# Hop of a transposed copy moved from its output to its input, with whole first loads on two queues and a new instruction order

## The chip, the cores and the metric

The kernel runs on one core of one Trainium2 chip. The metric is the device time of one execution in microseconds. The kernel before is known by three runs and by one profiled execution, from which all durations come.

## What is computed

The reference is a gated linear recurrence over 768 steps for 4 batches and 8 heads of 48 channels, followed by a two-layer network on the 3072 resulting rows of 384 channels.

```
f = 1.0 / (1.0 + np.exp(-f_logit))
state = np.zeros((B, H, D, D))
for t in range(S):                       # S = 768, D = 48
    state = f[:, :, t, :, None] * state + np.einsum('bhd,bhe->bhde', k[:, :, t], v[:, :, t])
    y[:, :, t] = np.einsum('bhd,bhde->bhe', q[:, :, t], state)
x = y.transpose(0, 2, 1, 3).reshape(B * S, H * D)
h = x @ w_in                             # 384 x 2048
out = np.maximum(0.01 * h, h) @ w_out    # 2048 x 384
```

All inputs and the output are float32; the kernel computes in bfloat16 with float32 sums.

## The kernel before

**Units.** The sequence is cut into 6 chunks of 128 steps; a chunk of one batch is a unit, so there are 24 units, numbered chunk by chunk (units 0 to 3 are the first chunks of the four batches). Within a unit the recurrence becomes matmuls: the log gates are summed by a triangular matrix (`gate_pe`), k and q are scaled by exponentials of these sums (`decay_em`, `decay_a`, `k_scale`, `q_scale`), both are transposed on TensorE (`turn_pe`) and copied out of PSUM (`turn_k`, `turn_q`), multiplied into scores (`score_pe`), masked (`mask_dve`), multiplied with v and with the state of the chunk before (`mix_pe`), and the state is carried on (`state_pe`, `state_dve`, `state_pool`). The result goes out of PSUM (`y_out`), is transposed (`x_pe`, `x_out`) into `xT`, and the network follows per pair of units: `up` (w_in, eight calls of 6 matmuls a pair, into PSUM), `up_act` (leaky ReLU on ACT into `gT`), `down` (w_out) and `put`, which copies the rows out of PSUM and stores them. For the first four units `down_cols` and `put_cols` do the second layer in two halves of the columns of w_out.

**The first chunks.** Units 0 to 3 are done together, in a layout of their own whose helpers begin with `q_`. Partition 32 groups of 4 steps by 4 batches: partition p holds batch p % 4, and four consecutive steps j lie in one row. `load_quad` (L67) loads f, k and q of one batch into every fourth partition. The heads are done in two halves hh of four. `q_turn_pe` (L211) transposes the scaled k or q into a PSUM bank; there the columns lie in the order pair of heads, j, group of steps t, batch b. `kTq` and `qTq` want them as pair of heads, batch, step (t, j). `q_turn_out` (L217) makes the two access patterns of the copy between them, and `q_k_out` and `q_q_out` run it through `move` on VectorE (L140) or ScalarE (L138), one copy of 128 x 512 for each half of heads and pair pp. `q_score_pe` (L228) reads the copies of both pairs of one half; `q_mask`, `q_wf_act` with `q_mask_pool`, `q_mix_pe`, `y_out`, `x_pe` and `x_out` follow. `q_back_pe` turns k back for the state.

**Order.** The order is written out by hand as one long list of calls; no scheduler moves anything. Each call puts its instructions at the end of the queue of its engine (V is VectorE or DVE, A is ScalarE or ACT, G is GpSimd or POOL), and each engine runs its queue in order. All loads (`load_part`, L155) and all outputs (`put`, `put_cols`) are issued by SyncE's queue (SP), in order as well, so a load that stands behind an output is issued only when that output's data are ready. The weights (`load_w_in` in four parts, `load_w_out` in two halves) are issued by POOL and converted to bfloat16 on the way. Raw loads have rings of six buffers. Each load or output by SP or ACT also waits for the one eight places earlier to have landed. `idle_pe(n, bank)` (L130) issues n matmuls on zeros whose result nobody reads. PSUM has eight banks; the last number of a call is its bank.

In the list before, the four calls of `load_part(4, ...)` are followed on SP by `put_cols(0, 0, 1)`, the load of f of unit 5, `put_cols(1, 0, 2)`, and the loads of k, q and v of unit 5. The first `up` calls are `up(0, 0, 7)`, `up(0, 1, 5)` and `up(0, 5, 4)`; eleven `up` stand ahead of the first `down_cols`.

Of the kernel before, what the change touches and what calls it, by code (L numbers as in the profile page):

```python
# [9 lines left out]
FP32 = mybir.dt.float32  # L10
# [6 lines left out]
def kernel(  # L17
# [45 lines left out]
    fq = [const.tile([128, 4, 4, D], FP32, name=f"fq{i}", tag=f"fq{i}") for i in range(2)]  # L63
    kq = const.tile([128, H, 4, D], FP32, tag="kq")
    qq = [const.tile([128, 4, 4, D], FP32, name=f"qq{i}", tag=f"qq{i}") for i in range(2)]

    def load_quad(eng, t, src, b, lo, n):  # L67
        eng.dma_start(out=t[b::4, :, :, :].rearrange("p h j d -> p h (j d)"),
                      in_=src[b, lo:lo + n, 0:C, :].rearrange("h (t j) d -> t h (j d)", j=4))
# [12 lines left out]

    nc.scalar.preload_act_table_set("natural_log_exp_and_others")
# [27 lines left out]
    qhs = [const.tile([128, H, 64], BF16, name=f"qh{i}", tag=f"qh{i}") for i in range(3)]  # L111
    khs = [const.tile([128, H, 64], BF16, name=f"kh{i}", tag=f"kh{i}") for i in range(4)]
# [12 lines left out]
    for t in lfs + khs + qhs:  # L125
        nc.vector.memset(t[:, :, D:64], 0.0)
    for t in state_b:
        nc.vector.memset(t, 0.0)
# [19 lines left out]
    turned = {name: ring(name, 3, [128, P2, 128], BF16) for name in ("kT", "qT")}  # L148
# [36 lines left out]
    def q_exp_act(hh):  # L185
        nc.scalar.activation(fq[hh], fq[hh], AF.Exp, scale=-1.0)

    def q_ln_act(hh):
        nc.scalar.activation(lfq[hh][:, :, :, 0:D], fq[hh].rearrange("p h j d -> p j h d"), AF.Ln, bias=1.0)
# [18 lines left out]
    def q_q_scale(eng, hh, a):  # L208
        q_scale_half(eng, qhq, qq[hh], aq, hh, a)
# [104 lines left out]
    def q_scale(u):  # L314
        r = raw[u]
        nc.gpsimd.tensor_mul(qhs[u % 3][:, :, 0:D], r["q"], a_ts[u % 3])  # L316
# [4 lines left out]
    def turn_pe(u, bk):  # L321
        tp = bank16(bk).rearrange("p (i a n) -> p i a n", i=2, a=P2)
        for i, src in enumerate((khs[u % 4], qhs[u % 3])):
            for p in range(P2):
                nc.tensor.transpose(tp[:, i, p, :], src[:, 2 * p:2 * p + 2, :], ident)  # L325

# [112 lines left out]
    idle_pe(31, 7)  # L439
# [3 lines left out]
    q_gate_pe(0, 0, 0)  # L443
    q_gate_pe(0, 1, 1)
    q_ln_act(1)
    idle_pe(3, 7)
    q_decay_act(0, 1, emq, 1.0, 1)
    q_end_pe(2)
    q_gate_pe(1, 0, 3)
    q_decay_act(0, 0, emq, 1.0, 0)  # L450
    q_k_scale(V, 0, 1)
    q_end_act(2)
    q_k_scale(V, 0, 0)
    q_gate_pe(1, 1, 4)
    q_decay_act(0, 0, aq, -1.0, 0)
    q_decay_act(0, 1, aq, -1.0, 1)
    q_q_scale(V, 0, 0)
    q_turn_pe(khq, 0, 0, 5)
    q_turn_pe(khq, 0, 1, 5)
    q_decay_act(1, 1, emq, 1.0, 4)  # L460
    q_q_scale(G, 0, 1)
    q_turn_pe(qhq, 0, 0, 6)
    q_k_out(V, 0, 0, 5)
    idle_pe(4, 7)
    q_decay_act(1, 1, aq, -1.0, 4)
    q_decay_act(1, 0, emq, 1.0, 3)
    q_k_scale(G, 1, 1)
    q_k_out(V, 0, 1, 5)
    q_turn_pe(qhq, 0, 1, 6)
    idle_pe(7, 7)  # L470
    q_decay_act(1, 0, aq, -1.0, 3)
    q_k_scale(V, 1, 0)
    q_q_out(A, 0, 0, 6)
    q_q_scale(G, 1, 0)
    cast_v(V, 0)
    q_turn_pe(khq, 1, 0, 7)
    q_q_out(A, 0, 1, 6)
    q_turn_pe(khq, 1, 1, 7)
    q_q_scale(V, 1, 1)
    load_w_in(0)  # L480
    q_turn_pe(qhq, 1, 0, 2)
    q_k_out(V, 1, 0, 7)
    q_score_pe(0, 1, 0, 1)
    load_w_in(1)
    q_turn_pe(qhq, 1, 1, 2)
    q_wf_act(0, 1, 0, 0)
    q_k_out(V, 1, 1, 7)
    q_score_pe(0, 0, 4, 5)
    cast_v(G, 1)
    idle_pe(2, 6)  # L490
    q_q_out(A, 1, 0, 2)
    cast_v(G, 2)
    q_mask(0, 1, 1, 1)
    q_back_pe(3, 3)
    idle_pe(6, 7)
    q_mask_pool(0, 1, 0)
    q_q_out(A, 1, 1, 2)
    q_mask(0, 0, 1, 5)
    q_score_pe(1, 0, 6, 0)
    q_mask(0, 0, 0, 4)  # L500
    idle_pe(3, 7)
    load_w_in(2)
    q_mask(1, 0, 0, 6)
    q_score_pe(1, 1, 7, 1)
    load_w_in(3)
    idle_pe(7, 5)
    q_wf_act(1, 1, 1, 1)
    load_w_out(0)
    q_mask(1, 0, 1, 0)
    q_wf_act(1, 1, 0, 7)  # L510
    q_back_out(V, 3, 3)
    q_mix_pe(0, 2)
    q_mask_pool(1, 1, 1)
    q_mix_pe(1, 5)
    q_back_pe(0, 4)
    y_out(A, 0, 2)
    y_out(V, 1, 5)
    idle_pe(2, 7)
    q_back_out(A, 0, 4)
    x_pe(0, 6)  # L520
    x_pe(1, 1)
# [84 lines left out]
    state_dve(4)
    turn_q(4, 1)
    down_cols(2, 0, 0)
    load_part(5, "v", v)
    put_cols(3, 0, 6)  # L610
    load_part(6, "f", f_logit)
    score_pe(4, 7, 3)
    put_cols(2, 0, 0)
    down_cols(3, 1, 2)
    mask_dve(4, 1, 3)
    load_part(6, "k", k)
    mask_dve(4, 0, 7)
    gate_exp(5)
    down_cols(0, 1, 5)
    load_part(6, "q", q)  # L620
    put_cols(3, 1, 2)
    gate_ln(5)
    load_part(6, "v", v)
    mix_pe(4, 4)
    put_cols(0, 1, 5)
    gate_pe(5, 1)
    state_pool(4)
    y_out(A, 4, 4)
    down_cols(2, 1, 6)
    load_part(7, "f", f_logit)  # L630
    decay_em(5, 1)
    decay_a(5, 1)
    k_scale(5)
    load_part(7, "k", k)
    x_pe(4, 0)
    down_cols(1, 1, 3)
    put_cols(2, 1, 6)
    x_out(V, 4, 0)
    gate_exp(6)
    q_scale(5)  # L640
    load_part(7, "q", q)
    gate_ln(6)
    up_one(4, 3, 7)
    cast_v(G, 5)
    put_cols(1, 1, 3)
    load_part(7, "v", v)
    turn_pe(5, 2)
    up_one_act(4, 3, 7)
    up_one(4, 1, 5)
    turn_k(5, 2)  # L650
    load_part(8, "f", f_logit)
    turn_q(5, 2)
    up_one(4, 0, 4)
    up_one_act(4, 1, 5)
    cast_v(G, 6)
    gate_pe(6, 1)
    load_part(8, "k", k)
    up_one_act(4, 0, 4)
    score_pe(5, 6, 0)
    up_one(4, 2, 3)  # L660
    decay_em(6, 1)
    mask_dve(5, 0, 6)
    load_part(8, "q", q)
    gate_exp(7)
    k_scale(6)
    down(4, 0, 7)
    mask_dve(5, 1, 0)
    gate_ln(7)
    load_part(8, "v", v)
    up_one_act(4, 2, 3)  # L670
    mix_pe(5, 2)
    decay_a(6, 1)
    state_pe(6, 5)
    gate_pe(7, 4)
    load_part(9, "f", f_logit)
    state_dve(6)
    down(4, 1, 7)
    y_out(A, 5, 2)
    q_scale(6)
    decay_em(7, 4)  # L680
    load_part(9, "k", k)
    decay_a(7, 4)
    cast_v(G, 7)
    x_pe(5, 6)
    turn_pe(6, 0)
    put(4, 7)
    k_scale(7)
    gate_exp(8)
    state_pe(5, 3)
    load_part(9, "q", q)  # L690
    x_out(V, 5, 6)
    gate_ln(8)
    turn_k(6, 0)
    up_one(5, 3, 1)
    q_scale(7)
    state_dve(5)
# [640 lines left out]
```

## Time and profile before

| | us |
|---|---|
| median of three runs (203.01, 203.26, 205.38) | 203.26 |
| profiled execution, device time | 203.25 |
| its span, first to last instruction | 201.5 |
| TensorE (PE) busy | 186.6 |
| ScalarE (ACT) busy | 120.6 |
| VectorE (DVE) busy | 96.5 |
| GpSimd (POOL) busy | 82.1 |

Mean granted TensorE clock: 0.971. A busy PE is not a PE at its peak, since matmuls overlap and their ends are modelled; the zero matmuls of `idle_pe` (65 of them, 13.4 us) are counted as busy. Shares over the whole span mix stages, so the busy strip (40 slices of 5.04 us) and the timeline say more than the sums. In timeline lines the first two columns are start and length of a piece in us, x2 the number of instructions in it; a name after an arrow in square brackets is what ended the idle time before it. PEld is the weight load of a matmul, SPq a queue's issue of a DMA.

### The profile page before, as it was taken

Reading aid. Unit: us, or ns where it says so; the run is one execution under the profiler, and the core shown is the slowest. Engines: PE = TensorE matmul, PEld = TensorE weight load, DVE = VectorE, ACT = ScalarE, POOL = GpSimd, SP = SyncE. Lnnn points to the kernel's source line nnn. Section 1 sums busy time; section 2 is a strip of 40 time slices with the busy share of each in tenths; the row PEclk is TensorE's granted clock in tenths of the full one; section 3 lists DMA queues with packets and bytes.
Section 4 is the critical chain, followed back from the end, with each engine's and each line's share of the span. In section 5 each row is a group of like instructions: output and inputs, shape, how many; then the busy total and the mean of one; then the engine's idle time right before and its main releaser. Section 6 shows DMA issues by size and latency. Waiting matters only on the chain.

```text
span 201.5 us, 5284 instructions
## 1 busy us (share of the span) xinstructions
PE 186.6 (93%) x2094; PEld 146.6 (73%) x2094; DVE 96.5 (48%) x215; ACT 120.6 (60%) x237; POOL 82.1 (41%) x144
## 2 busy tenths in 40 slices
PE   4993599999999979999999999999999999999991
PEld 3782368999997748787778767877878877776660
DVE  6069955405445836954656456333555460111221
ACT  2678935883456768768778666766656734343200
POOL 4046742442444768795467581671632000000000
PEclk9998559999999999999999999999999999999998
DMA  4878999099988999999999899722100011111121
GB/s 130 239 179 129 221 195 164 0 89 226 199 195 183 233 190 235 185 217 188 219 192 235 174 229 204 160 47 74 42 0 3 0 42 39 39 39 42 41 108 50
DMA packets 100537, 27.08 MB, mean 134 GB/s; under 512 B 92320, under 2 KB 100512, under 8 KB 100512
## 3 DMA queue, kind: packets, MB, share of 16 engines
q1 hardware_dynamic: 94208, 23.21, 52.5%
q0 software_dynamic: 5728, 3.15, 11.8%
q10 hardware_dynamic: 576, 0.39, 0.8%
q8 instruction: 16, 0.26, 0.5%
q14 instruction: 9, 0.07, 0.1%
HBM read 25.17 MB, written 4.72 MB: 148 GB/s over the span
## 4 chain that ended last, share of the span: by engine, by line
PE 78%; DVE 6%; DMA 6%; POOL 3%; issue 3%; SPq 2%; ACT 1%; POOLq 0%; DVEq 0%; ACTq 0%
PE ps L402 29%; PE ps L416 23%; PE ps L132 5%; DVE kTq L140 4%; PE ps L325 4%; PE ps L427 3%; PE ps L341 3%; DMA v_raw<-in_v_dram 2%; DMA k_raw<-in_k_dram 2%; DMA f_raw<-in_f_logit_dram 2%; PE ps L385 2%; PE ps L354 2%; PE ps L351 1%; PE ps L362 1%; PE ps L194 1%
## 5 line engine op out<-in xcount | busy, mean ns | idle before, releaser
L411 ACT ACTIVATE gT<-ps 128x512 bf16<-128x512 f32 x88 | 52.1, 597 | 33.8 <-PE ps L402 31.7
L402 PE MATMUL ps<-xT,w_in_b 128*128 128x256 bf16 x528 | 67.8, 273 | 0.2 <-DVE xT L140 0.2
L416 PE MATMUL ps<-w_out_b,gT 128*128 128x384 bf16 x320 | 56.9, 326 | 0.0
L402 PEld LDWEIGHTS <-w_in_b 128*128 128x128 bf16 x528 | 49.1, 98 | 8.0 <-issue 0.3
L416 PEld LDWEIGHTS <-gT 128*128 128x128 bf16 x320 | 30.3, 98 | 17.2
L344 DVE TENSOR_TENSOR wm<-ps,ut 128x512 bf16<-128x512 f32 x40 | 25.9, 686 | 11.1 <-PE ps L341 9.4
L422 DVE COPY osb<-ps 128x384 f32<-128x384 f32 x20 | 11.1, 557 | 37.1 <-PE ps L416 37.1
L312 POOL TENSOR_TENSOR kh<-k_raw,em_t 128x384 bf16<-128x384 f32 x20 | 18.1, 913 | 12.1 <-ACT em_t L304 5.2
L281 POOL CAST sb<-sf 64x192 bf16<-64x192 f32 x40 | 13.6, 341 | 22.8 <-PE ps L351 14.8
L316 POOL TENSOR_TENSOR qh<-q_raw,a_t 128x384 bf16<-128x384 f32 x20 | 18.1, 911 | 4.7 <-ACT a_end L309 1.4
L140 POOL CAST v_b<-v_raw 128x384 bf16<-128x384 f32 x23 | 11.8, 512 | 13.9 <-DMA v_raw<-in_v_dram 10.2
L328 DVE COPY kT<-ps 128x512 bf16<-128x512 bf16 x20 | 8.5, 423 | 16.3 <-PE ps L325 12.7
L288 ACT ACTIVATE f_raw<-f_raw 128x384 f32<-128x384 f32 x20 | 10.5, 526 | 9.4 <-DMA f_raw<-in_f_logit_dram 9.4
L138 ACT CAST xn<-ps 128x384 bf16<-128x384 f32 x21 | 10.0, 480 | 9.6 <-PE ps L354 8.6
L132 PE MATMUL ps<-fill 128*128 128x256 bf16 x65 | 13.4, 373 | 1.1 <-DVE ind L124 1.1
L140 DVE COPY xT<-ps 128x384 bf16<-128x384 bf16 x22 | 7.7, 352 | 8.7 <-PE ps L385 4.7
L427 PE MATMUL ps<-w_out_b,gT 128*128 128x192 bf16 x128 | 11.5, 246 | 0.0
L132 PEld LDWEIGHTS <-fill 128*128 128x128 bf16 x65 | 8.0, 129 | 4.4 <-issue 1.9
L304 ACT ACTIVATE em_t<-ps 128x384 bf16<-128x384 f32 x20 | 9.9, 495 | 2.1 <-PE ps L300 1.4
L291 ACT ACTIVATE lf<-f_raw 128x384 bf16<-128x384 f32 x20 | 10.5, 524 | 0.5
L427 PEld LDWEIGHTS <-gT 128*128 128x128 bf16 x128 | 10.5, 98 | 0.1
L307 ACT ACTIVATE a_t<-ps 128x384 bf16<-128x384 f32 x20 | 9.8, 495 | 0.0
(92 smaller groups left out, 240.5 us busy)
## 6 DMA issues: line engine op xcount, KB each, us to landing
v_raw<-in_v_dram SPq DMA_DIRECT2D x24, 192.0 KB, 3.9
f_raw<-in_f_logit_dram SPq DMA_DIRECT2D x20, 192.0 KB, 3.9
k_raw<-in_k_dram SPq DMA_DIRECT2D x20, 192.0 KB, 4.0
q_raw<-in_q_dram SPq DMA_DIRECT2D x20, 192.0 KB, 3.9
out_dram<-osb SPq DMA_DIRECT2D x20, 192.0 KB, 1.9
w_in_b<-in_moe_w_in_dram POOLq DMA_DIRECT2D x4, 384.0 KB, 7.2
w_out_b<-in_moe_w_out_dram POOLq DMA_DIRECT2D x2, 768.0 KB, 11.3
kq<-in_k_dram SPq DMA_DIRECT2D x4, 192.0 KB, 3.8
```

The source lines that it names most:

```text
L132: nc.tensor.matmul(bank(bk)[:, 0:256], fill[:, 0:128], fill[:, 0:256], start=True, stop=True)
L140: eng.tensor_copy(out=out, in_=in_)
L281: nc.gpsimd.tensor_copy(out=state_b[b][r, :, e * D:(e + 1) * D], in_=state_f[b][r])
L288: nc.scalar.activation(raw[u]["f"], raw[u]["f"], AF.Exp, scale=-1.0)
L312: nc.gpsimd.tensor_mul(khs[u % 4][:, :, 0:D], raw[u]["k"], em_ts[u % 3])
L316: nc.gpsimd.tensor_mul(qhs[u % 3][:, :, 0:D], r["q"], a_ts[u % 3])
L344: nc.vector.tensor_mul(wms[e][u % 3], bank(bk).rearrange("p (i n) -> p i n", i=P2), ut[:, None, :].to_broadcast([128, P2, 128]))
L402: nc.tensor.matmul(bank(bk)[:, i * 256:(i + 1) * 256], w_in_b[:, kk, ff * 128:(ff + 1) * 128], xTs[m % 3][:, kk].rearrange("p a n -> p (a ...
L411: nc.scalar.activation(gTs[m % GBUFS][:, 2 * g:2 * g + 2].rearrange("p f a n -> p (f a n)"), bank(bk), AF.Prelu, alpha=0.01)
L416: nc.tensor.matmul(bank(bk)[:, 0:KD], gTs[u // 2 % GBUFS][:, ff, u % 2, :], w_out_b[:, ff, :], start=(ff == 0), stop=(ff == NF - 1))
L422: nc.vector.tensor_copy(out=osb, in_=bank(bk)[:, 0:KD])
L427: nc.tensor.matmul(bank(bk)[:, 0:CH], gTs[u // 2 % GBUFS][:, ff, u % 2, :], w_out_b[:, ff, half * CH:(half + 1) * CH], start=(ff == 0), st ...
```

## The change

Four things change in the helpers. `q_turn_out` builds its access patterns in the order of the destination: the copy now writes `kTq` or `qTq` consecutively and reads PSUM with hops of 256 bytes, where it read consecutively and wrote with hops. The first loads of f and q are whole per batch (eight heads) in place of two halves, and batches 2 and 3 of f and k are issued by ACT, on both sides of the loading of its function table. The buffers of scaled k and q, and those of their transposes, become halves of common tiles; the ring of scaled q grows from three to four. A helper `turn_dma` is added, which nothing calls.

The list of calls is written anew from its beginning to its end. The same calls are made as often as before, except that: `idle_pe` issues 81 matmuls (65 before); of the eight copies of turned k and q, DVE does three and ACT five (four and four); masks by DVE straight from PSUM are six (five) and those by way of ACT and POOL two (three); two casts of v are on DVE (one); all 24 `y_out` are on ACT (21). On SP three loads of unit 5 (f, k, q) stand ahead of the first output, and later loads stand further ahead of outputs. The first `up` is `up(0, 5, 5)`, which reads part 2 of w_in; sixteen `up` stand ahead of the first `down_cols`.

```
-    fq = [const.tile([128, 4, 4, D], FP32, name=f"fq{i}", tag=f"fq{i}") for i in range(2)]
+    fq = const.tile([128, H, 4, D], FP32, tag="fq")
...
-    for hh in range(2):
-        for b in (2, 3):
-            load_quad(nc.scalar, fq[hh], f_logit, b, 4 * hh, 4)
-    for hh in range(2):
+    for b in (2, 3):
+        load_quad(nc.scalar, fq, f_logit, b)
+    nc.scalar.preload_act_table_set("natural_log_exp_and_others")
+    for b in (2, 3):
+        load_quad(nc.scalar, kq, k, b)
+    for t, src in ((fq, f_logit), (kq, k)):
         for b in (0, 1):
-            load_quad(nc.sync, fq[hh], f_logit, b, 4 * hh, 4)
-    for b in range(B):
-        load_quad(nc.sync, kq, k, b, 0, H)
-    for hh in range(2):
-        for b in range(B):
-            load_quad(nc.sync, qq[hh], q, b, 4 * hh, 4)
-
-    nc.scalar.preload_act_table_set("natural_log_exp_and_others")
+            load_quad(nc.sync, t, src, b)
+    for b in range(B):
+        load_quad(nc.sync, qq, q, b)
...
     def q_turn_out(dst, hh, bk, pp):
-        tp = bank16(bk).rearrange("p (a j t b) -> p a j t b", a=2, j=4, b=4)
-        o = dst[hh].rearrange("p a b (t j) -> p a j t b", j=4)
-        return dict(out=o[:, pp], in_=tp[:, pp])
+        tp = bank16(bk).rearrange("p (a j t b) -> p a b t j", a=2, j=4, b=4)
+        return dict(out=dst[hh][:, pp].rearrange("p b (t j) -> p b t j", j=4), in_=tp[:, pp])
...
-    idle_pe(31, 7)
+    idle_pe(40, 7)
```

The calls of the new list around the copies and the first weights, in their order (others left out):

```
    q_k_scale(G, 0, 1)
...
    cast_v(G, 0)
...
    load_w_in(0)
...
    load_w_in(1)
...
    q_q_scale(G, 0, 0)
    q_k_out(A, 1, 0, 6)
    cast_v(V, 1)
...
    q_k_out(V, 0, 0, 5)
    q_k_out(A, 1, 1, 6)
    load_w_in(2)
...
    q_q_out(V, 1, 0, 7)
    idle_pe(11, 4)
    q_q_out(A, 0, 0, 0)
    cast_v(G, 3)
    cast_v(V, 2)
    load_w_in(3)
    q_q_out(A, 0, 1, 0)
    q_k_out(V, 0, 1, 5)
    q_q_out(A, 1, 1, 7)
    load_w_out(0)
    q_score_pe(0, 0, 3, 1)
...
    q_mix_pe(2, 2)
    q_mix_pe(3, 4)
    up(0, 5, 5)
```

More of the change, by code (lines that the diff above doesn't have):

```diff
@@ L466 @@
[L466 to L485, printed above, removed]
@@ L646 @@
[L646 to L654, printed above, removed]
-    cast_v(G, 6)
[L656 to L663, printed above, removed]
+    turn_pe(5, 6)
+    load_part(8, "k", k)
+    x_out(V, 4, 3)
+    decay_em(6, 4)
+    state_pe(5, 7)
@@ L670 @@
[L670 to L675, printed above, removed]
+    state_pe(6, 6)
+    up_one(4, 3, 5)
+    up_one_act(4, 1, 3)
     state_dve(6)
[L677 to L680, printed above, removed]
+    gate_pe(7, 7)
     load_part(9, "k", k)
-    decay_a(7, 4)
-    cast_v(G, 7)
[L684 to L690, printed above, removed]
@@ L838 @@
[L838 to L861 removed]
+    down(5, 1, 4)
@@ new lines @@
+    q_scale(12)
+    down(6, 0, 4)
+    gate_exp(13)
+    load_part(15, "f", f_logit)
+    gate_ln(13)
+    cast_v(G, 12)
+    turn_pe(11, 6)
+    gate_pe(13, 2)
+    load_part(15, "k", k)
+    turn_k(11, 6)
+    state_pe(12, 1)
+    x_pe(9, 5)
+    decay_em(13, 2)
+    mix_pe(10, 3)
+    turn_q(11, 6)
+    turn_pe(12, 0)
+    k_scale(13)
+    x_out(V, 9, 5)
+    load_part(15, "q", q)
+    y_out(A, 10, 3)
+    state_dve(12)
+    up(3, 6, 6)
+    cast_v(G, 13)
+    up(4, 2, 5)
+    turn_k(12, 0)
@@ new lines @@
+    decay_a(15, 5)
+    up(4, 0, 3)
+    load_part(17, "v", v)
+    mask_dve(13, 1, 1)
+    cast_v(G, 15)
+    up_act(4, 1, 4)
+    x_pe(10, 2)
+    mix_pe(11, 7)
+    q_scale(15)
+    x_out(V, 10, 2)
+    up_act(4, 0, 3)
+    state_pe(15, 0)
+    load_part(18, "f", f_logit)
+    up(4, 3, 5)
+    gate_exp(16)
+    state_pool(11)
+    mix_pe(13, 1)
+    load_part(18, "k", k)
+    up_act(4, 3, 5)
+    x_pe(12, 4)
+    turn_pe(15, 2)
+    x_out(V, 12, 4)
+    gate_ln(16)
+    down(8, 0, 3)
+    state_pool(13)
@@ L908 @@
+    state_dve(15)
+    load_part(18, "q", q)
+    y_out(A, 13, 1)
+    turn_k(15, 2)
+    decay_a(14, 6)
+    turn_q(15, 2)
+    cast_v(G, 16)
+    x_pe(13, 5)
+    load_part(18, "v", v)
+    state_pe(14, 4)
+    y_out(A, 11, 7)
+    up(4, 4, 0)
+    x_out(V, 13, 5)
+    q_scale(14)
+    gate_exp(17)
+    state_dve(14)
+    up(6, 3, 1)
+    load_part(19, "f", f_logit)
+    gate_ln(17)
+    x_pe(11, 6)
+    up_act(4, 4, 0)
     turn_pe(14, 2)
-    k_scale(15)
-    up_act(4, 2, 3)
-    x_pe(12, 7)
@@ new lines @@
+    mask_dve(15, 0, 4)
+    load_part(20, "q", q)
+    up(5, 4, 2)
+    decay_a(17, 7)
+    put(8, 3)
+    cast_v(G, 18)
+    x_pe(14, 5)
+    load_part(20, "v", v)
+    mix_pe(15, 1)
+    up_act(5, 4, 2)
+    q_scale(17)
+    x_out(V, 14, 5)
+    up(5, 5, 6)
+    y_out(A, 15, 1)
+    state_pool(15)
+    load_part(21, "f", f_logit)
+    up(6, 2, 0)
+    gate_exp(19)
+    up_act(5, 5, 6)
+    turn_pe(17, 4)
+    load_part(21, "k", k)
+    gate_pe(18, 7)
+    up_act(6, 2, 0)
+    turn_k(17, 4)
+    up(5, 7, 3)
@@ new lines @@
+    turn_q(17, 4)
+    decay_em(18, 7)
+    up(6, 1, 5)
+    load_part(21, "q", q)
+    decay_a(18, 7)
+    k_scale(18)
+    score_pe(17, 2, 1)
+    up_act(6, 1, 5)
+    x_pe(15, 6)
+    load_part(21, "v", v)
+    down(9, 0, 0)
+    mask_dve(17, 0, 2)
+    q_scale(18)
+    up_act(5, 7, 3)
+    x_out(V, 15, 6)
+    gate_exp(20)
+    load_part(22, "f", f_logit)
+    cast_v(G, 19)
+    mask_dve(17, 1, 1)
+    up(7, 5, 4)
+    gate_ln(20)
+    up(7, 1, 7)
+    up_act(7, 5, 4)
+    turn_pe(18, 5)
+    up_act(7, 1, 7)
@@ new lines @@
+    mask_dve(18, 1, 1)
+    gate_exp(22)
+    up(7, 3, 7)
+    up_act(7, 7, 5)
+    put(9, 0)
+    state_pe(18, 3)
+    mix_pe(18, 2)
+    up_act(7, 3, 7)
+    state_dve(18)
+    up(5, 3, 1)
+    y_out(A, 18, 2)
+    state_pool(18)
+    up(7, 2, 0)
+    up_act(5, 3, 1)
+    x_pe(18, 5)
+    up(6, 7, 7)
+    up_act(7, 2, 0)
+    decay_a(21, 4)
+    down(12, 0, 3)
+    up_act(6, 7, 7)
+    q_scale(21)
+    up(5, 0, 2)
+    up(6, 6, 1)
+    load_part(22, "v", v)
+    up_act(5, 0, 2)
+    turn_pe(21, 0)
@@ new lines @@
+    x_pe(21, 3)
+    x_pe(16, 7)
+    decay_a(19, 4)
+    mix_pe(20, 5)
+    x_out(V, 21, 3)
+    down(14, 1, 6)
+    x_out(V, 16, 7)
+    y_out(A, 20, 5)
+    q_scale(19)
+    up(8, 0, 1)
+    put(14, 6)
+    up(8, 1, 3)
+    up_act(8, 0, 1)
+    x_pe(20, 4)
+    up(8, 6, 7)
+    up_act(8, 1, 3)
+    x_out(V, 20, 4)
+    up(10, 3, 5)
+    up_act(8, 6, 7)
+    turn_pe(19, 6)
+    up_act(10, 3, 5)
+    up(10, 0, 1)
+    turn_k(19, 6)
+    q_scale(23)
+    turn_q(19, 6)
+    up(10, 7, 4)
+    up_act(10, 0, 1)
```

1343 lines of the change are left out of this document (608 added, 735 removed).

## The prediction

> **What bounds the kernel now.** I read the busy strip first, to find where TensorE is not full.
>
> ```profile
> PE   4993599999999979999999999999999999999991
> PEclk9998559999999999999999999999999999999998
> DMA  4878999099988999999999899722100011111121
> GB/s 130 239 179 129 221 195 164 0 89 226 199 195 183 233 190 235 185 217 188 219 192 235 174 229 204 160 47 74 42 0 3 0 42 39 39 39 42 41 108 50
> ```
>
> A slice is 5.04 us. From slice 6 (30 us) to the end PE is at 9 but for one slice, so the kernel is PE-bound there: it ends when its list of matmuls is done. The holes are in slices 3 and 4 (15 to 25 us), and slices 4 and 5 also have half the clock. PE busy in slices 1 and 2 is largely the zero matmuls of idle_pe, which compute nothing. So the time is: the moment T0 of the first matmul of up(), plus the PE list behind it, plus PE's gaps in it, plus the tail. The timeline gives T0 and what stands ahead of it:
>
> ```profile
> 14.30 4.74 ACT L138 COPY qTq<-ps 128x512 bf16<-128x512 bf16 x2
> 15.37 1.71 POOL L167 DMA_DIRECT2D w_in_b<-in_moe_w_in_dram  x2
> 19.30 4.68 DVE L140 COPY kTq<-ps 128x512 bf16<-128x512 bf16 x2
> 19.36 2.67 SPq L158 DMA_DIRECT2D q_raw<-in_q_dram  x1
> 20.36 4.70 ACT L138 COPY qTq<-ps 128x512 bf16<-128x512 bf16 x2
> 21.59 1.58 POOL L167 DMA_DIRECT2D w_in_b<-in_moe_w_in_dram  x2
> 22.07 2.43 SPq L158 DMA_DIRECT2D v_raw<-in_v_dram  x1
> 31.22 0.82 PE L402 MATMUL ps<-xT,w_in_b 128*128 128x256 bf16 x6 [0.22 <-DVE xT L140]
> 41.87 0.36 SPq L434 DMA_DIRECT2D out_dram<-osh  x1
> 74.61 0.32 PE L297 MATMUL ps<-lf,ut 128*128 128x384 bf16 x1 [1.18 <-ACT lf L291]
> ```
>
> T0 is 31.22. Ahead of it lie eight copies of turned k and q, four on DVE (two more from 13.25) and four on ACT, which end at 25.06. The tile views of kTq and qTq give their price, the page's groups that of copies of the same size that write plain rows:
>
> ```profile
> L140 DVE COPY kTq<-ps x4: 2414/2535/2642, 13.2 to 21.3; 128x512 bf16<-128x512 bf16 x4
> L138 ACT COPY qTq<-ps x4: 2429/2616/2827, 14.3 to 22.3; 128x512 bf16<-128x512 bf16 x4
> ```
> ```profile
> L328 DVE COPY kT<-ps 128x512 bf16<-128x512 bf16 x20 | 8.5, 423 | 16.3 <-PE ps L325 12.7
> L344 DVE TENSOR_TENSOR wm<-ps,ut 128x512 bf16<-128x512 f32 x40 | 25.9, 686 | 11.1 <-PE ps L341 9.4
> L411 ACT ACTIVATE gT<-ps 128x512 bf16<-128x512 f32 x88 | 52.1, 597 | 33.8 <-PE ps L402 31.7
> ```
>
> 2.35 us each (4.70 for two) against 0.42 to 0.69 us: q_turn_out hops 256 bytes between neighbouring elements of its output, and both engines pay 4.6 ns an element for it.
>
> Two more views: how long the weights take to land (tile w_in_b), and what a hole does to the clock (two windows).
>
> ```profile
> DMA to landing us min/median/max: 5.6/7.2/8.0
> ```
> ```profile
> 14.86:18.39 3.53, 0.00 (x0) 0.00 (x1) 3.53 (x4) 3.53 (x2) 3.15 (x5) 1.00 0.71 108
> 24.00:29.40 5.40, 5.36 (x47) 3.41 (x48) 3.31 (x6) 2.13 (x3) 1.59 (x3) 0.50 1.25 214
> ```
>
> After 3.53 us with no matmul the clock is 0.50 from about 19.4, and it stays there through 5.4 us of full PE work.
>
> The sum is made against the profiled execution: span 201.5, time 203.25, so 1.75 around the span. 203.25 is the median of the runs (203.26).
>
> **The change, part by part.** *The copies.* q_turn_out now hops in its reading of PSUM and writes in order. No row shows a hopping read of PSUM. Lowest: 0.42 (L328, nothing hops). Highest: 2.35, the hop costs the same on the other side. I take 0.69 on DVE and 0.60 on ACT (L344, L411: one element at a time), because those engines' plain f32 reads already go at that pace and the rows put the penalty on the only side that hopped.
>
> The Trainium skill speaks against this: SBUF — State Buffer (section Door 1: The DMA port swizzle) and PSUM — Partial Sum Buffer (Specifications) say that SBUF has 16-byte lines and PSUM 8-byte ones, and that crossing lines costs. By that a read that crosses a line at each element need not be cheaper than the write was; no run here shows it, and it is the third rival below.
>
> *Up to the copies.* idle_pe(31) took 6.39 us and ends at 9.39; nine more at 0.11 (three took 0.33 at 10.72) end at 10.4. f_logit now comes in four whole loads, issued by 2.2 us; with 3.7 to landing, and 2 x 0.9 us of exp and ln, ln(0) ends at 7.8, hidden under the fill. Gates 1.32, fill and end sums 0.7, gates 1.34: 13.8 (12.8 before). The last decays end at 15.1, q_q_scale(1,1), the last on DVE, at 15.9 (0.55 each), and the transposes of k that the first copy on ACT reads at 16.0.
> *Copies.* ACT has five now, 16.0 to about 19.0; DVE has three and two casts of v (0.66), 15.9 to 19.3. Before, the last ended at 25.06.
> *Behind them.* Six masks on DVE at 0.69 (19.7 to 23.9; before five, and three on ACT and POOL, now two), mix, y_out, x_pe, x_out (0.2 + 0.5 + 0.2 + 0.5): both halves of xT0 lie ready at 24.5. That is 6.7 us before 31.22.
>
> *Weights.* The first up() is up(0,5), which needs load_w_in(2), and a matmul list runs in order. Before, the four w_in issues were at 15.4 to 23.2 and long done. Now POOL issues them behind q_k_scale (ends 12.6) and cast_v(0) (13.2): parts 0 and 1 from 13.4, part 2 at 16.2, part 3 at 17.5, w_out behind it. DMA does the rest. Rates: from 16.4 to 35.2 (then 0 GB/s) DMA moved four unit loads, four parts of w_in and half of w_out. A unit load is 0.97 us of all engines (192 KB at 203 GB/s, the window 81 to 101 us), so 18.8 - 3.9 = 14.9 us for weights, by bytes 2.5 us a part and 5.0 for half of w_out. While weights flowed SP needed 2.43 us for a unit load (v_raw above), so SP's queue gets 0.97/2.43 = 0.4 of DMA and POOL's 0.6. Check: the first part would land 2.5/0.6 = 4.2 us after its start; the fastest took 5.6 from issue, so 1.4 for starting and finishing. Now SP's queue never runs dry there, since unit 4 and f, k, q of unit 5 (7 loads, none behind an output) are issued by about 15 us. Three parts: 13.4 + 1.4 + 7.5/0.6 = 27.3. So T0 is about 27.2, by weights and not by copies: **-4.0 us**. Bounds: POOL's queue served alone, 22.3, and then the copies' 24.5 holds; an equal split, 29.8.
>
> This cover means that a copy at 1.1 us (five on ACT, 2.5 us later) costs nothing.
>
> *Moved ahead of T0.* mix of batches 2 and 3 (0.20 each) and state_pe(3) (0.17): **-0.6**. The number of other matmuls behind T0 is the same (88 up, 40 down, 20 turn_pe and so on); the 16 added zero matmuls all lie ahead of it.
> *Loads ahead of outputs.* SP stood still from 24.5 to 41.87 behind the first output. Now three loads of unit 5 go ahead of it, and k of unit 6 (51.52) follows the second output, at about 42 (T0 + 16 up of 0.66 + 1.3 of other work + down_cols 1.32 = 40.3 for the first). PE's gaps behind T0 sum to 2.06 us (0.02, 0.13, 0.30, 1.57, 0.04 in the windows); the largest waits for a late f (the line at 74.61), two more for q. I take half: **-1.0**, between 0 and -2.1.
> *w_out.* Half 0 is down by about 37 and wanted at 39.0; half 1 is issued near 36.6, lands by 43 and is wanted at 45.2. Hidden, with some 2 us to spare each; if that is gone, PE waits the difference.
> *At nothing:* eight fewer issues on SP and ACT (0.65 each; q arrives before its scale by either), the merged rings (same instructions; memsets under DVE's idle time to 11.3), three y_out moved to ACT (0.5 each; ACT is 60% busy).
>
> Sum: 203.25 - 4.0 - 0.6 - 1.0 = 197.65, say **197.7**.
>
> **Rivals.**
> *Copies set T0, not weights.* For it: rows give the 0.4/0.6 split only while SP has one load in hand. Against: now SP has seven. T0 24.5: 203.25 - 6.7 - 0.6 - 1.0 = 195.0. Chance 0.20.
> *The wait for weights drops the clock.* PE stands from 24.5 to 27.2, 2.7 us; the hole that dropped it was 3.53. If it drops, up() begins at half speed for 5.4 us as from 24.0 to 29.4: + 2.7, 200.4. Chance 0.13.
> TensorE: Matmul & The Clock Gate (Part 1, What's actually happening), of the Trainium skill, has the clock fall after an idle window of about 3.4 us; the 3.53 row agrees. By that rule T0 up to 27.9 keeps the clock.
> *The hop costs on the read side too* (slower). ACT's five copies in a row set it, since the scores of heads 4 to 7 need the last. At 2.35 us they end at 27.8 in place of 19.0, scores come 8.2 later and T0 at 32.7. PE would then stand from 18.3 to past 25, more than 3.53, so the clock drops as it did before: some 0.9 more on the path (scores 0.61 in place of 0.33, mix and turns likewise), T0 33.6, and the first up() at half speed, + 2.7. 203.25 + 2.4 + 2.7 - 0.6 - 1.0 = 206.7; at 3.3 us, 211. It is slower than before from about 2.2 us a copy. For it: both engines paid the same 4.6 ns, as if the memory set it; against: only the writing side hopped. Chance 0.12.
> *The new order gives the gain back.* The whole list behind T0 is new, and it may starve PE elsewhere: gaps of 6 us in place of 2, 203. For it: the first down_cols, which lets the first output and all loads behind it go, stood behind 11 up() and stands behind 16 now, 3.3 us later against T0; against: every load from f of unit 5 on is issued earlier. Chance 0.07.
>
> **How the numbers follow.** The forecast has the other 0.48. Its own range is 193.9 (T0 24.5, all gaps gone) to 201.2 (T0 29.8, no gap gone); with the slower rivals it reaches to 203.0, and below 194.5 I leave one in twenty. 2% is 4.1 us, about what a measurement of this kernel can tell from no change, so faster means under 199.2. Forecast: 0.39 of its 0.48; first rival 0.20; the clock 0.05; the rest 0.02. Faster 0.66, same 0.28, slower 0.06.
>
> **What would show it.** Right: kTq and qTq copies at 0.55 to 0.75 us, the last done near 19.3; the first L405 matmul near 27 with its wait put down to w_in_b; clock 1.0 through slices 3 to 5; k of unit 6 issued before 45. Wrong: copies over 1.2 us; T0 under 25.5 or over 30; PE gaps behind T0 over 3 us in sum.

## The result and the profile after

The changed kernel takes 194.51 us (median of 4; 193.79 to 194.70), the kernel before beside it 203.13 (median of 4): ratio 0.959, 95% interval 0.953 to 0.965. It is faster by 8.6 us. Forecast were 197.7 us and a faster kernel; the time that came is close to that of the first rival, 195.0. The profiled execution took 193.79 us with a span of 191.9, so 1.9 lie around the span (1.75 before). Ratios, here and below, compare the fast runs of two kernels, medians are of all their runs, and the profiled run of the kernel with the hop on its output again is one of its slower ones.

The busy strip of the page; a slice is now 4.80 us:

```profile
PE   4997989999999999999999999999999999999991
...
PEclk9999999999999999999999999999999999999999
DMA  5999999999899999999998955472110100021211
GB/s 153 323 209 157 188 175 176 131 230 198 188 189 207 219 196 202 226 182 234 209 212 172 236 110 117 92 171 77 44 41 3 41 3 0 9 77 43 82 68 55
```

The holes of slices 3 and 4 are all but closed (7 and 9 tenths busy), the clock is at 0.9 or more in every slice (mean 0.998), and the 0 GB/s of slice 7 (35 to 40 us), when SP stood behind the first output, has become 131. The timeline has the moment at which the first `up` begins and what stands before it (L405 is the `up` line of the new file, L137 and L139 are the copies of `move` on ACT and DVE):

```profile
12.69 1.70 POOL L167 DMA_DIRECT2D w_in_b<-in_moe_w_in_dram  x2
...
15.21 4.64 SPq L158 DMA_DIRECT2D v_raw<-in_v_dram  x1
...
15.53 0.80 POOL L167 DMA_DIRECT2D w_in_b<-in_moe_w_in_dram  x1
...
17.55 1.56 ACT L137 COPY qTq<-ps 128x512 bf16<-128x512 bf16 x3 [1.17 <-PE ps L215]
...
22.99 0.86 ACT L137 COPY xT<-ps 128x384 bf16<-128x384 bf16 x2
...
23.40 0.56 PE L249 MATMUL ps<-v_b,wmq 128*128 128x48 bf16 x16
...
23.79 0.86 ACT L137 CAST xn<-ps 128x384 bf16<-128x384 f32 x2
...
24.67 0.55 PEld L405 LDWEIGHTS <-w_in_b 128*128 128x128 bf16 x6 [0.82 <-DMA w_in_b<-in_moe_w_in_dram]
24.67 0.83 PE L405 MATMUL ps<-xT,w_in_b 128*128 128x256 bf16 x6 [0.71 <-ACT xn L137]
...
40.87 0.88 SPq L158 DMA_DIRECT2D k_raw<-in_k_dram  x1
```

T0 is 24.67 in place of 31.22. The two lines of 24.67 name two releasers for one instant: the matmul ACT's `xn` (done at 24.65), the weight load part 2 of w_in. The list of calls tells them apart. This `xn` row is `y_out` of units 2 and 3, out of banks 2 and 4, while `up(0, 5, 5)` writes bank 5 and reads `xT` of units 0 and 1, so it needs neither. Its own `xT` was complete at 23.85, and the matmuls ahead of it ended at 23.96. Part 2, issued at 15.53, landed 9.1 us later, at 24.6. In this run the weights came last, by 0.7 us. The last matmul ends at 187.8, so 163.1 us lie between T0 and the end of the list (before: 197.2 less 31.22, that is 166.0).

The tiles of the copies, and beside them `kqh`, whose copies turn k back for the state and read PSUM without a hop:

```profile
L137 ACT COPY kTq<-ps x2: 586/589/592, 15.3 to 15.8; 128x512 bf16<-128x512 bf16 x2
L139 DVE COPY kTq<-ps x2: 678/678/678, 16.5 to 17.9; 128x512 bf16<-128x512 bf16 x2
...
L137 ACT COPY qTq<-ps x3: 585/592/605, 17.6 to 18.5; 128x512 bf16<-128x512 bf16 x3
L139 DVE COPY qTq<-ps x1: 675/675/675, 17.1 to 17.1; 128x512 bf16<-128x512 bf16 x1
...
L137 ACT COPY kqh<-ps x2: 592/592/592, 19.6 to 21.1; 128x512 bf16<-128x512 bf16 x2
L139 DVE COPY kqh<-ps x2: 424/425/426, 23.8 to 31.5; 128x512 bf16<-128x512 bf16 x2
```

The three numbers are shortest, median and longest in ns. On ACT a read that hops 256 bytes costs what a plain read costs (592); on DVE 678 in place of 425. On the output the same hop had cost 2535 (DVE) and 2616 (ACT).

### The profile page after: what moved, and what is told of

The parts are those of the page before. It is cut to its first block, busy times and chain, and to the rows that moved or that the text cites. A ratio compares the mean times of both kernels' runs of the same rounds, so it can differ in the third digit from the quotient of the medians.

```text
span 191.9 us, 5307 instructions
## 1 busy us (share of the span) xinstructions
PE 182.9 (95%) x2110; PEld 145.5 (76%) x2110; DVE 90.2 (47%) x210; ACT 114.6 (60%) x241; POOL 79.9 (42%) x141
## 3 DMA queue, kind: packets, MB, share of 16 engines
HBM read 25.17 MB, written 4.72 MB: 156 GB/s over the span
## 4 chain that ended last, share of the span: by engine, by line
PE 91%; ACT 2%; DVE 2%; issue 1%; POOL 1%; POOLq 0%
PE ps L405 31%; PE ps L419 27%; PE ps L430 6%; PE ps L131 5%; PE ps L324 4%; PE ps L344 3%; PE ps L388 2%; PE ps L398 2%; PE ps L357 2%; PE ps L354 2%; PE ps L296 2%; PE ps L365 2%; PE ps L194 1%; DVE qhq L203 1%; PE ps L232 1%
## 5 line engine op out<-in xcount | busy, mean ns | idle before, releaser
L405 PE MATMUL ps<-xT,w_in_b 128*128 128x256 bf16 x528 | 66.4, 273 | 0.7 <-ACT xn L137 0.7
L405 PEld LDWEIGHTS <-w_in_b 128*128 128x128 bf16 x528 | 49.1, 98 | 7.9 <-DMA w_in_b<-in_moe_w_in_dram 0.8
L347 DVE TENSOR_TENSOR wm<-ps,ut 128x512 bf16<-128x512 f32 x40 | 26.0, 686 | 13.5 <-PE ps L344 4.5
L311 POOL TENSOR_TENSOR kqh<-k_raw,em_t 128x384 bf16<-128x384 f32 x20 | 18.3, 913 | 18.5 <-ACT em_t L303 10.5
L331 DVE COPY kqT<-ps 128x512 bf16<-128x512 bf16 x40 | 15.2, 419 | 19.6 <-PE ps L324 19.3
L315 POOL TENSOR_TENSOR kqh<-q_raw,a_t 128x384 bf16<-128x384 f32 x20 | 18.3, 913 | 6.9 <-issue 5.4
L137 ACT CAST xn<-ps 128x384 bf16<-128x384 f32 x24 | 11.2, 479 | 14.3 <-DVE osh L436 7.5
L131 PE MATMUL ps<-fill 128*128 128x256 bf16 x81 | 12.7, 303 | 1.1 <-DVE ind L121 1.1
L139 POOL CAST v_b<-v_raw 128x384 bf16<-128x384 f32 x22 | 11.3, 514 | 5.0 <-DMA v_raw<-in_v_dram 2.5
L139 DVE COPY xT<-ps 128x384 bf16<-128x384 bf16 x22 | 7.7, 355 | 11.8 <-PE ps L388 7.0
L324 PE MATMUL ps<-ident,kqh 128*128 128x128 bf16 x160 | 12.2, 219 | 0.0
```

Of the source, the lines that this page charges most:

```text
L131: nc.tensor.matmul(bank(bk)[:, 0:256], fill[:, 0:128], fill[:, 0:256], start=True, stop=True)
L139: eng.tensor_copy(out=out, in_=in_)
L311: nc.gpsimd.tensor_mul(khs[u % 4][:, :, 0:D], raw[u]["k"], em_ts[u % 3])
L315: nc.gpsimd.tensor_mul(qhs[u % 4][:, :, 0:D], r["q"], a_ts[u % 3])
L331: nc.vector.tensor_copy(out=turned[name][u % 3], in_=bank16(bk).rearrange("p (i a n) -> p i a n", i=2, a=P2)[:, i])
L347: nc.vector.tensor_mul(wms[e][u % 3], bank(bk).rearrange("p (i n) -> p i n", i=P2), ut[:, None, :].to_broadcast([128, P2, 128]))
```

## The experiments

T0 and the time behind it (end of the last matmul less T0) are from the profiled run of each kernel; the ratio is to runs of the kernel before on the same chip. Chips differed by about 2 us in the kernel before, so between chips the ratios are what may be compared.

| kernel | T0 | behind T0 | median | ratio, 95% |
|---|---|---|---|---|
| before | 31.22 | 166.0 | 203.13 | 1 |
| changed | 24.67 | 163.1 | 194.51 | 0.959 [0.953, 0.965] |
| changed, again | 25.23 | 165.5 | 195.54 | 0.954 [0.944, 0.963] |
| hop on the output again | 33.94 | 166.8 | 205.21 | 1.005 [0.999, 1.011] |
| old kernel, new copies | 23.66 | 171.8 | 202.34 | 0.990 [0.981, 0.998] |
| old first loads | 28.76 | 164.2 | 198.44 | 0.977 [0.960, 0.994] |
| unit 5's loads behind output | 24.58 | 169.3 | 199.97 | 0.982 [0.970, 0.995] |
| first `up` on part 0 | 24.52 | 166.4 | 195.44 | 0.956 [0.948, 0.965] |
| hop of 8 bytes | 25.64 | 165.3 | 198.30 | 0.967 [0.958, 0.976] |
| old kernel, copies and loads | 22.74 | 170.1 | 201.39 | 0.977 [0.964, 0.990] |
| one scale to DVE | 25.33 | 163.1 | 195.65 | 0.965 [0.957, 0.973] |
| two scales to DVE, part 0 | 22.86 | 164.3 | 194.65 | 0.955 [0.949, 0.961] |

**Hop on the output again.** The changed kernel, with the old `q_turn_out` alone:

```
-        tp = bank16(bk).rearrange("p (a j t b) -> p a b t j", a=2, j=4, b=4)
-        return dict(out=dst[hh][:, pp].rearrange("p b (t j) -> p b t j", j=4), in_=tp[:, pp])
+        tp = bank16(bk).rearrange("p (a j t b) -> p a j t b", a=2, j=4, b=4)
+        o = dst[hh].rearrange("p a b (t j) -> p a j t b", j=4)
+        return dict(out=o[:, pp], in_=tp[:, pp])
```

> The changed kernel with only the copy of turned k and q put back to its old direction (reads in order, writes with hops). Theory A, the copies set the first up(): ACT's five copies take 5 x 2.35 us in place of 5 x 0.6, so the first up() moves from 24.7 us to 32 or later, PE's clock drops to 0.5 in the hole, and the time is 202 to 206 us, the gain of the change gone. Theory B, the new list and the earlier loads made the gain and the copies lay beside other work: first up() before 27 us, time under 197 us.

The whole gain is gone, as theory A said. The timeline of that run shows TensorE waiting for ACT's copies in a row, and the windows what this does to the clock (columns: stretch, length, busy time of PE, PEld, DVE, ACT and POOL with their counts, clock, DMA share, GB/s):

```profile
22.37 0.23 PE L233 MATMUL ps<-qTq,kTq 64*128 64x128 bf16 x2 [3.69 <-ACT qTq L137]
24.64 0.51 PE L233 MATMUL ps<-qTq,kTq 64*128 64x128 bf16 x6 [2.03 <-ACT qTq L137]
...
26.91 0.51 PE L233 MATMUL ps<-qTq,kTq 64*128 64x128 bf16 x6 [1.00 <-ACT qTq L137]
...
33.94 0.82 PE L406 MATMUL ps<-xT,w_in_b 128*128 128x256 bf16 x6
```
```profile
22.40:33.90 11.50, 8.47 (x99) 6.06 (x99) 6.32 (x10) 8.28 (x11) 2.98 (x4) 0.55 1.33 181
33.90:38.00 4.10, 4.10 (x47) 3.67 (x44) 1.39 (x4) 3.23 (x7) 0.29 (x1) 1.00 0.42 81
```

The copies take 2.44 to 2.85 us here. So the copy's access pattern is necessary for all that the other parts bring.

**Old kernel, new copies.** The kernel before, with the new `q_turn_out` and nothing else (the diff above in reverse).

> The kernel before with only the new direction of the copy. Theory A: copies of 0.6 to 0.69 us, first up() at 24 to 26 us in place of 31.2, but the loads still stand behind the first output, so that PE's gaps behind it grow from 2.1 us to 3 to 5: time 196.5 to 199.5 us, between two thirds and nine tenths of the gain. Theory B: time over 200 us.

The first half came as theory A said: T0 falls by 7.6 us. The time falls by about 1% only, less than either bound of A; the time is theory B's. The waits of PE behind T0 show where the gain went:

```profile
25.48 0.27 PE L249 MATMUL ps<-v_b,wmq 128*128 128x48 bf16 x4 [0.90 <-POOL wmq L239]
28.51 0.83 PE L401 MATMUL ps<-xT,w_in_b 128*128 128x256 bf16 x6 [2.10 <-DMA w_in_b<-in_moe_w_in_dram]
31.22 1.49 PE L401 MATMUL ps<-xT,w_in_b 128*128 128x256 bf16 x12 [0.68 <-DMA w_in_b<-in_moe_w_in_dram]
37.18 1.49 PE L426 MATMUL ps<-w_out_b,gT 128*128 128x192 bf16 x16 [0.47 <-DMA w_out_b<-in_moe_w_out_dram]
```

The old list issues the weights from 16.6 and 20.4 on, which was early enough for a T0 of 31 and is late for one of 23.7; the matmuls behind T0 take 5.8 us longer, of which these four waits are 4.2 (two for w_in, one for w_out, one for a mask on POOL).

**Old first loads.** The changed kernel with the first loads of before: f and q in halves, all of k and q on SP.

```
-    fq = const.tile([128, H, 4, D], FP32, tag="fq")
+    fq = [const.tile([128, 4, 4, D], FP32, name=f"fq{i}", tag=f"fq{i}") for i in range(2)]
...
-    for b in (2, 3):
-        load_quad(nc.scalar, fq, f_logit, b)
...
+    for hh in range(2):
+        for b in (2, 3):
+            load_quad(nc.scalar, fq[hh], f_logit, b, 4 * hh, 4)
```

> The changed kernel with the first loads of f, k and q as before (f and q in halves of four heads, k all by SP, the function table loaded behind four issues on ACT). Theory A: f arrives at about the same time; q is issued up to 4 us later and its last quarter lands near 12.5 us, and v0 to v3 and all that SP issues behind it some 3 to 4 us later, so that POOL issues w_in later: first up() 1 to 3 us later, time 195.5 to 198 us. Theory C, that the whole first loads are worth nothing since the same bytes pass the same 16 engines: time within 0.5 us of the changed kernel, 194 to 195 us.

T0 is 28.76, 3.5 to 4.1 us later than in the two profiles of the changed kernel, and theory C falls by this; the ratio's interval still touches that of the changed kernel. What holds POOL is v of unit 0: it stands behind q on SP and is issued from 12.03 on, in the changed kernel from 7.87. POOL's cast waits for it, and POOL in turn holds two things, the weights and its product of q, on which transposes wait:

```profile
16.16 0.50 POOL L142 CAST v_b<-v_raw 128x384 bf16<-128x384 f32 x1 [3.59 <-DMA v_raw<-in_v_dram]
...
18.33 1.02 POOL L206 TENSOR_TENSOR qhq<-qq,aq 128x384 bf16<-128x384 f32 x1
...
19.31 0.80 POOL L170 DMA_DIRECT2D w_in_b<-in_moe_w_in_dram  x1
...
19.41 1.04 PE L218 MATMUL ps<-ident,qhq 128*128 128x128 bf16 x8 [2.77 <-POOL qhq L206]
...
28.76 0.83 PE L408 MATMUL ps<-xT,w_in_b 128*128 128x256 bf16 x6 [0.80 <-DMA w_in_b<-in_moe_w_in_dram]
```

My prediction gave the whole loads no price of their own ("at nothing: eight fewer issues"). This run also puts all of k back on SP, so it does not tell the whole loads from the second queue.

**Unit 5's loads behind the first output.** The changed kernel with f, k and q of unit 5 moved back behind `put_cols` of the first output:

```
-    load_part(5, "f", f_logit)
...
-    load_part(5, "k", k)
...
-    load_part(5, "q", q)
...
+    load_part(5, "f", f_logit)
+    load_part(5, "k", k)
+    load_part(5, "q", q)
```

> The changed kernel with the loads of f, k and q of unit 5 put behind the first output on SP, where the kernel before had them. Theory D, loads ahead of outputs pay behind the first up(): that first up() comes at 23.9 to 24.7 us, but PE's gaps behind it grow from 0.3 us to 1.5 to 3, time 195.5 to 197.5 us. Theory E, the loads only took DMA from the weights and their lead is not used: w_in part 2 lands before the first up() is ready, time 193 to 194.5 us.

T0 stays (24.58), and the ratio goes to 0.982 from 0.959 and 0.954, about 5 us (the intervals lie apart). Theory D holds, and by more than it said. The waits of PE behind T0 in the two profiles, first of this kernel, then of the changed kernel's second run (columns: total, times, longest):

```profile
PE ps L296 <- ACT lf L290: 4.0, 6, 1.1
PE ps L398 <- DVE xT L139: 1.0, 1, 1.0
```
```profile
PE ps L296 <- ACT lf L290: 1.8, 2, 1.3
PE ps L357 <- DVE wm L347: 0.3, 1, 0.3
```

**The changed kernel again,** to set the next three beside it on their chip: no edit. T0 is 25.23, half a microsecond later than in the first run, with 1.8 us of waits for f that the first run did not have. The profiles of one kernel differ by that much. They differ in what comes last, too:

```profile
24.31 0.86 ACT L137 COPY xT<-ps 128x384 bf16<-128x384 bf16 x2
...
25.11 0.86 ACT L137 CAST xn<-ps 128x384 bf16<-128x384 f32 x2
...
25.23 0.81 PE L405 MATMUL ps<-xT,w_in_b 128*128 128x256 bf16 x6
```

The first `up` begins while `xn` runs, so it does not wait for it. Part 2 of w_in landed at 24.8 (issued at 15.67, 9.1 to landing), `xT` was complete at 25.17, and no wait for weights is left: here the chain of copies, masks, mix and `x_out` comes last, by 0.4 us.

> The changed kernel once more, on the chip of the other experiments and beside the kernel before there. All theories expect first up() at 24.7 us and a ratio near 0.96 of the kernel before.

**First `up` on part 0.** `up(0, 5)` and `up(0, 0)` change places, so that the first `up` needs the part of w_in that is issued first.

```
-    up(0, 5, 5)
+    up(0, 0, 5)
...
-    up(0, 0, 1)
+    up(0, 5, 1)
```

> The changed kernel with up(0, 5) and up(0, 0) exchanged, so that the first up() reads part 0 of w_in (landed at 19.4 us) in place of part 2 (24.6). Theory F, part 2 of w_in and nothing else sets the first up(): it comes at 23.9 us in place of 24.7, with no wait put down to w_in_b, 0.7 us less in all, 193 to 194 us where the changed kernel has 194.5. Theory G, the copy of xT0 on ACT is as late as part 2: first up() at 24.4 to 24.7, time the same within 0.3 us.

No wait for weights is left at T0, and T0 is 24.52 all the same. But the copies' chain was itself later in this profile than in the changed kernel's first: the masks on DVE begin at 19.70 against 19.08, and `xT` is complete at 24.47 against 23.85. So the chain sets T0 here, and what the exchange alone is worth this T0 does not say. The medians on this chip are the same (195.44 and 195.54), so theory F's 0.7 us do not show in the time. Taken together, the chain and part 2 of w_in come within a microsecond of each other, and which of them is last changes from profile to profile; with unit 5's loads behind the output it was the weights (0.39 us of wait).

**A hop of 8 bytes on both sides.** The copy walks t last in place of j, so that neighbouring elements are 8 bytes apart in reading and in writing.

```
-        tp = bank16(bk).rearrange("p (a j t b) -> p a b t j", a=2, j=4, b=4)
-        return dict(out=dst[hh][:, pp].rearrange("p b (t j) -> p b t j", j=4), in_=tp[:, pp])
+        tp = bank16(bk).rearrange("p (a j t b) -> p a b j t", a=2, j=4, b=4)
+        return dict(out=dst[hh][:, pp].rearrange("p b (t j) -> p b j t", j=4), in_=tp[:, pp])
```

> The changed kernel with the copy of turned k and q going through the steps of one batch in a third order: hops of 8 bytes on both sides, in place of 256 bytes on the input and none on the output. Theory H, what cost 4.6 ns an element before was that each 2-byte element was written apart from its neighbour, however near: copies of 2.35 us again, first up() near 33 us, time 203 to 206 us. Theory I, it was the 256-byte hop, each element in another line: with 8 bytes half of a 16-byte line is written at a time, copies of 0.6 to 1.3 us, first up() before 27 us, time 194 to 197 us.

```profile
L137 ACT COPY kTq<-ps x2: 1313/1363/1413, 15.2 to 16.2; 128x512 bf16<-128x512 bf16 x2
L139 DVE COPY kTq<-ps x2: 1270/1282/1294, 16.4 to 18.9; 128x512 bf16<-128x512 bf16 x2
```

At 2.5 ns an element it stands between the copy in order (1.15 on ACT) and the hop of 256 bytes on the output (5.0, from 2535 ns): the distance counts, not only the breaking of a run. (The read hops 8 bytes here too; that this costs nothing is taken from the read with hops of 256 and was not tried alone.) The durations miss theory I's bound by a little and H's by far; T0 (25.64) is I's, 0.4 us over the changed kernel beside it. Its median is 2.8 us higher, but the two intervals overlap, and the profiled runs (196.98 and 196.75) do not show where that would lie; this stays open.

**Old kernel, new copies and unit 5's loads ahead.** The kernel before with both edits.

> The kernel before with the new direction of the copy, and f, k and q of unit 5 loaded ahead of the first output. Theory J, the gain of the copy alone (first up() 7.6 us earlier, time only 1.7 us less in the profiled run) was given back because SP stood behind the first output: PE's gaps behind the first up() for f, q and gT fall from about 2.7 us to under 1, time 196 to 199 us against 201.6. Theory K, it was given back to the weights alone (three waits of 3.3 us for w_in and w_out), which three more loads only delay: time 201 to 203 us.

It falls between J and K. T0 is 22.74, and PE's waits behind it for f, q and gT fall to 0.8 us, as J says; but then come 2.09 us of wait for w_in and 1.01 for w_out, as K says. The median is in K's range, the profiled run (198.95) in J's. Loads ahead are worth about 5 us in the new list; in the old one, with the weights late, the ratio is better by 0.013 (some 2.6 us), but the intervals overlap, so no gain from them is shown there.

**Scales from POOL to DVE.** In the changed kernel DVE's products run slower while POOL runs one. POOL has two of the eight scales there; the kernel before had three, so the new list had itself moved one scale of q to DVE (and one `q_back_out` from DVE to ACT). Here first one of POOL's two goes to DVE, then both, with part 0 for the first `up`:

```
-    q_q_scale(G, 0, 0)
+    q_q_scale(V, 0, 0)
```

> The changed kernel with one scale of q, q_q_scale(0, 0), on DVE in place of POOL. In all runs of the changed kernel two or three of DVE's six scales took 0.85 to 1.57 us in place of 0.55, at times when POOL ran a scale or cast of its own. Theory L, a DVE product of two SBUF operands stands still while POOL's own runs: with POOL's scale gone, DVE's scales between 13.5 and 16 us take 0.55 each, DVE does one more and still reaches its first copy 0.5 to 1 us sooner, POOL issues part 2 of w_in 1 us sooner, and first up() comes at 23.8 to 24.3 us; time 0.3 to 0.9 us less than the changed kernel. Theory M, the slow ones wait for something else (DMA writes of w_in and of loads): they stay slow, the added scale costs 0.55 us, first up() 0.3 to 0.6 us later.

```
-    q_k_scale(G, 0, 1)
+    q_k_scale(V, 0, 1)
...
-    q_q_scale(G, 0, 0)
+    q_q_scale(V, 0, 0)
...
-    up(0, 5, 5)
+    up(0, 0, 5)
```

> The changed kernel with both of POOL's scales of the first chunks on DVE and up(0, 5) exchanged with up(0, 0), so that neither POOL's work nor part 2 of w_in stands ahead of the first up(). Theory L: eight scales of 0.55 us on DVE without a slow one, first up() at 23.3 to 24.2 us, time 0.5 to 1.4 us less than the changed kernel. Theory M: slow scales remain, two more of them on DVE, first up() later than 25 us and time the same or more.

Theory L holds for the products: with one scale moved, those between 13.5 and 16 us take 0.55 to 0.56 each. The tile of qhq in the changed kernel, then in the one with both scales on DVE:

```profile
L203 DVE TENSOR_TENSOR qhq<-qq,aq x3: 544/560/1551, 11.4 to 14.7; 128x384 bf16<-128x384 f32 x3
L203 POOL TENSOR_TENSOR qhq<-qq,aq x1: 1165/1165/1165, 14.4 to 14.4; 128x384 bf16<-128x384 f32 x1
```
```profile
L203 DVE TENSOR_TENSOR qhq<-qq,aq x4: 551/554/559, 11.2 to 14.6; 128x384 bf16<-128x384 f32 x4
```

Its T0 and its time were not met. With one moved, T0 is 25.33, for the weights set it (1.66 us of wait for part 2 of w_in); with both moved and part 0 first it is 22.86, sooner than forecast. The profiled run of that last version took 193.05, the shortest of all, but its median of 194.65 is not apart from the changed kernel's 194.51 and 195.54: no version beats the changed kernel by more than the runs can tell.

## Why the prediction came out as it did

**The steps that held.** Copies: 0.69 and 0.60 forecast, 0.68 and 0.59 measured; the last done at 19.1 (17.55 + 1.56) against 19.3. Part of that agreement is luck: forty zero matmuls were done at 9.29 and not at 10.4, and two of DVE's products, 1.11 and 1.55 us in place of 0.55, took the time back. The chain behind them: "both halves of xT0 lie ready at 24.5" against 23.9 and 25.2 in the two profiles. The clock stays up. k of unit 6 issued at 40.87, forecast "about 42". The hop on the output as the lock on everything: with it back the whole gain is gone.

**The step that failed: "SP's queue gets 0.97/2.43 = 0.4 of DMA and POOL's 0.6".** It put part 2 of w_in at 27.3 and T0 at 27.2. Part 2 was issued at 15.53 and landed 9.1 us later, at 24.6. I had read the rate of SP's queue from how long an issue took on SP; the rate is in the bytes that each queue moved. The tile v_raw, of the kernel before and then of the changed one:

```profile
L158 SPq DMA_DIRECT2D v_raw<-in_v_dram x24: 378/732/2764, 11.7 to 127.6; - x24
DMA to landing us min/median/max: 2.9/3.9/11.0
```
```profile
L158 SPq DMA_DIRECT2D v_raw<-in_v_dram x24: 368/658/4637, 7.9 to 126.3; - x24
DMA to landing us min/median/max: 3.0/3.9/17.2
```

The 11.0 is the load issued at 22.07 in the profile before, amid the weights: not 2.43 us but 11 passed until it was there, and it stood in the profile that I had. After, the load issued at 15.21 took 17.2. The two queues of the profile after from 16.0 to 34.4, while the weights flowed (q0 carries the weights, q1 what SP issues; packets, MB, and the time of the packets as a share of 16 engines, in which packets overlap):

```profile
q0 software_dynamic: 3530, 2.22, 82.2%
q1 hardware_dynamic: 5654, 1.07, 43.3%
```

1.07 MB are 5.4 unit loads; at 0.97 us of all engines each that is 5.3 of 18.4 us, a share of 0.29. The second profile gives 0.25, and the profile before, which I had, 0.26 (1.00 MB from 16.4 to 35.2). With 0.71 for POOL and the first issue at 12.7, where it came, the prediction's own formula gives 12.7 + 1.4 + 7.5/0.71 = 24.7, against 24.6. Nor were the seven loads issued by about 15 us: the last of them, q of unit 5, was issued at 29.31.

So T0 lies where the first rival, "copies set T0, not weights", had it, but only the second profile has that rival's mechanism. In the first the weights came last, as forecast, 2.7 us sooner than forecast. That the weights and the copies come out so close together is luck. With the T0 of the two profiled runs and the other terms as they were, the sum is 203.25 - 6.55 - 1.6 = 195.1 and 203.25 - 5.99 - 1.6 = 195.7, against medians of 194.51 and 195.54. The two are easily parted: with one scale moved to DVE the wait for the weights was 1.66 us.

**A term with the right size for the wrong reason: loads ahead of outputs, -1.0.** Behind T0 the profiles show -2.9 and -0.5 against before, where -1.6 was forecast for this and the matmuls moved ahead together, so the runs do not contradict the number. But I had taken it as half of the 2.06 us of gaps that were there. Without it the kernel has about 5 us more. My reading is that a T0 that is 6.6 us earlier also wants unit 5 and its successors 6.6 us earlier; the waits for f in that run (4.0 us against 1.8) fit it. The same holds for the first loads, priced at nothing and worth about 4 us of T0. The terms of the sum do not add: the copies alone are worth 1%, and the loads ahead, the whole first loads and the early weights each keep some of what the copies open.

**The rivals.** *The clock drops in the wait for weights:* the wait in the changed kernel was 0.7 us and not 2.7, and the clock stayed; in a neighbour a wait of 2.09 us dropped it (below). *The hop costs on the reading side:* not on ACT, by a quarter of a microsecond on DVE. The line sizes that the Trainium skill gives in SBUF — State Buffer (Door 1: The DMA port swizzle) and PSUM — Partial Sum Buffer (Specifications) do not show in ACT's reads (0.59 us with and without the hop), and what makes DVE's dearer is not shown; on the writing side the copies do get dearer from 8 to 256 bytes. *The new order gives the gain back:* the new one does not, but the old one does, as the copies in the old kernel show. I had weighed this danger for the wrong list.

## What to carry to other kernels

When an early stage becomes shorter, ask of every load and every weight behind it whether it comes that much earlier too; if not, the gain reappears as waits, and a part that looks worthless in the profile before (here whole loads, loads ahead of an output) is what keeps it. The share of a DMA queue is read from the bytes it moved under the same load, not from how long an issue holds its engine. When two chains end within a microsecond, one profile does not say which of them sets the pace, and the releaser that a line names has to agree with the list of calls. Where a copy must permute as here, let the reading side of PSUM hop and the writing side go in order, and try it by itself first: the price per element of both sides is one tile view away.

## What the runs showed of the hardware

- Price of a 128 x 512 copy of bfloat16 out of PSUM: 0.59 us on ACT and 0.42 on DVE in order on both sides; 0.59 and 0.68 when the read hops 256 bytes; 1.27 to 1.41 when both sides hop 8 bytes; 2.41 to 2.85 when the write hops 256.
- A product on DVE of two operands in SBUF takes 0.55 us alone and up to 1.56 while POOL runs one of its own (1.17 in place of 0.91). With POOL's two gone, all eight took 0.55 to 0.56, with POOL's DMA issues still beside them. The Trainium skill has this in SBUF — State Buffer (Who interferes with whom): a DVE instruction with two SBUF inputs contends with a GpSimd instruction that reads SBUF, and one of them blocks; the trace agrees (0.55 + 0.92 is 1.47; in the changed kernel's second run, with a POOL product of 0.92 beside it, the longest took 1.56).
- Loads on SP's queue got 0.25 and 0.29 of DMA in the two profiles, reckoned from bytes, while weights that are converted on the way were queued on POOL's; one load took 17.2 us to land in place of the median of 3.9.
- A shorter hole than 3.5 us can drop the clock, and the same hole need not. In the old kernel with copies and loads ahead, PE waited 2.09 us up to 26.79 and the clock was 0.50 from 28 to 31 (the window lines below); with the copies alone it waited 2.10 up to 28.51 and stayed at 1.00. The Trainium skill's idle window of about 3.4 us (TensorE: Matmul & The Clock Gate, Part 1, What's actually happening) does not foretell the first of these; what tells the two apart stays open. The columns are stretch, length, PE busy with its matmuls, clock, DMA share and GB/s.

```profile
25.00:26.00 1.00, 0.00 (x0) 1.00 1.21 189
26.00:27.00 1.00, 0.21 (x2) 1.00 1.25 204
27.00:28.00 1.00, 1.00 (x11) 0.79 1.16 180
28.00:29.00 1.00, 1.00 (x7) 0.50 1.33 173
```
